# One kernel, five edits: the kv turn by transposes, the last attention step and the row of expert blocks laid anew

## The chip, the cores and the metric

The kernel runs on one core of a Trainium2 chip. The metric is device time: microseconds (us) from start to end of one execution, the median over several runs. The engines are named as in the profile: PE is TensorE's matmuls, PEld its loads of weights (the stationary operand), DVE is VectorE, ACT ScalarE, POOL GpSimd, SP SyncE, which here only issues DMAs. A q behind a name (SPq, POOLq) is that engine's queue of DMA issues and waits.

## The reference, cut to what matters

```python
# q, k, v: B=8, H=8, S=576, Dh=64; omega: M=128 random features
def phi(x):
    proj = einsum('bhsd,md->bhsm', x, omega)
    return concatenate([cos(proj), sin(proj)], -1) / sqrt(m)
kv  = einsum('bhsm,bhsd->bhmd', phi(k), v);  z = sum(phi(k), axis=s)
num = einsum('bhsm,bhmd->bhsd', phi(q), kv)
den = einsum('bhsm,bhm->bhs', phi(q), z)        # held away from zero
x = (num / den) as rows                          # N = B*S = 4608 tokens of 512
# experts: E=8, w1 (512 x 1024), w2 (1024 x 512)
logits = normalized(x) @ normalized(expert_emb).T / tau
expert = argmax(logits);  gate = softmax(logits)[expert]
out = gate * (relu(x @ w1[expert]) @ w2[expert])
```

## The kernel before, in words

**Attention: 32 steps.** A step n is one pair of heads of one batch (8 batches, NPAIR = 4 pairs). PE's order in a step n is written out by hand: the projection of q of step n, the output product `num` (line 373) of step n-1, the projection of k of step n+2, the turn of k of step n+3, `kv_products` of step n+1 and `kv_turn` of step n. The other engines follow in the order in which the calls stand: ScalarE moves projections out of PSUM and takes sines and cosines (`wave`, line 297), VectorE takes the fractional turns (line 278), folds them (`fold`, line 284) and copies PSUM, POOL adds up the sums over s (`zsum`, lines 309 to 314).

**kv_turn.** `kv_products` leaves kv with the 64 entries of a head's rows down the partitions, sine and cosine one above the other; VectorE copies it into `kvT`. `kv_turn` (lines 341 and 348) then turns it so that features lie on the partitions, and at the same time multiplies it by the normalized expert embeddings, to get logits along with the outputs. It does both by one product for each of two heads: the 128x128 `kvT` is the stationary operand, and `rmat`, 144 columns (2 x (64 + 8)), moves. `rmat` holds for each pair a unit block of 64 (which turns) and a block of 8 embedding columns. The unit blocks are written once at the start by POOL (`set_up_unit`, 8 copies, line 542), the embeddings by VectorE (`set_up_turn`). A second product of `zs` with the two columns of `zmask` turns the sums. All are fp32. `kv_out` copies the outcome from PSUM (`kvnew`) into SBUF as the weights of `num`.

**Rows.** `norm` divides and leaves rows in `xrow`; `store_rows` (line 425) writes them to DRAM as two DMAs of 288 KB for each two steps, and `store_logits` adds logits and token numbers, from which tokens are later fetched.

**Experts: blocks of 128 tokens of one expert.** `NBLK` is 43, of which NMAIN = 40 always run. Routing is done in two parts: blocks 0 to 10 hold tokens of the first batches, and blocks from K1 = 11 on those of the rest, whose places come out of `route_second` during blocks 1 to 6. For a block j, `gather` (POOL, line 910) fetches the rows by an indirect DMA into one of XBUF = 3 buffers; `ready` casts them to fp16 (`cast`, line 945 on ScalarE, 947 on POOL; a small copy of the logits on POOL comes with it) and turns them by a transposing DMA on SP's queue (line 1016); `square` (ScalarE, line 955) and `power` (POOL, line 964), `score`, `tanh` and `weigh` make the gate; `hidden_products` (line 1054, 32 matmuls, weights addressed by register) is the first layer, `clamp` its relu (the first half on ScalarE, line 1067, the second on VectorE, line 1069, or also on ScalarE in the first eight turns of the loop), `result_products` (line 1087, 8 matmuls) the second layer, `result_out` scales by the gate on ScalarE (line 1102) and scatters on POOL (line 1103). `square` frees the gather's buffer.

**The row of blocks** is one loop over j. Each turn issues, in this order: `hidden(j+1)` with its clamp, `score(j+1)` in odd j, `ready(j+4)` (cast on POOL for j+4 below 11, then on ScalarE), `result_products(j)`, `result_out(j)`, `square(j+4)`, `gather(j+6)`. In turn 1, the rows of the last pair of steps are stored on ScalarE's queue and its logits on SP's. An engine goes through its instructions in that order and waits in place.

**Change of stage.** The last step is written out ahead of the loop: `num(last - 1)`, sine of q, `hidden_products(0)` on PE, then `kv_turn(last)`, `fold` and cosine, `hot(0)` (a one-hot compare on VectorE, line 850, wanted by the routing of the second part), `kv_out(last)` on VectorE, and `num(last)`.

**PSUM** is one tile of eight banks of 512 words. The first layer of block 0 writes banks 0 and 1; `kvnew` lies at the end of bank 7, beside `num`'s bank.

## Time and profile before

| what | value |
|---|---|
| median of 3 runs | 453.14 us (452.38 to 454.96) |
| the profiled execution | 451.52 us, span 449.7 us |
| busy PE, PEld | 432.5 us (96%), 356.4 us (79%) |
| busy DVE, ACT, POOL | 327.5 us (73%), 344.0 us (76%), 370.0 us (82%) |
| moved by DMA | 80.32 MB, mean 179 GB/s |
| DMAs issued by POOL | 32 pieces of weights of 512 KB, 40 gathers, 40 scatters |

The span runs from the first instruction to the last; the execution's own time also has what lies around it, 1.8 us here. Busy times come from the instructions' own records; a matmul's end is modelled, so that a busy PE isn't PE at its peak. In rows of a timeline the first two numbers are start and length in us; a group of instructions one after the other is drawn into one row with its count (x2), and in brackets stands how long the engine stood idle before it and what it had waited for.

### The profile page before, as it was taken

What the parts mean: (1) busy time and instruction counts of PE and PEld (TensorE: products, weight loads), DVE (VectorE), ACT (ScalarE), POOL (GpSimd) and SP (SyncE); (2) the same over time, 40 slices, a digit from 0 to 9 for tenths busy, and PEclk for the clock granted to TensorE, in tenths of its full rate; (3) what the DMA queues carried; (4) which work ended last, traced back from release to release, by engine and by line L of the source; (5) the groups of instructions that cost most, each with busy time, mean ns of one, the idle gap of its engine ahead of it and who ended that gap; (6) DMA issues with size and microseconds to landing.
All of it is one profiled execution on the core that took longest, in us unless ns stands there. A gap on an engine that the chain in (4) does not pass through costs nothing. (4 is left out here: it accounts for less than half of the span.)

```text
span 449.7 us, 18881 instructions
## 1 busy us (share of the span) xinstructions
PE 432.5 (96%) x7799; PEld 356.4 (79%) x7799; DVE 327.5 (73%) x735; ACT 344.0 (76%) x478; POOL 370.0 (82%) x507
## 2 busy tenths in 40 slices
PE   8999999999999999999999999998999999999992
PEld 4788888989888888889888888876767777777770
DVE  5679977788777789898899989999753554554450
ACT  4878988888888889888888888875556777676741
POOL 8999998988889888889899898987877778777741
PEclk9999999999999999999999999999999999999997
DMA  7999998999999989999898896559577767777530
GB/s 193 200 203 206 205 202 195 194 182 212 200 195 209 197 191 202 188 212 192 176 229 190 177 203 111 102 123 204 149 161 200 183 147 202 164 202 168 151 91 30
DMA packets 80390, 80.32 MB, mean 179 GB/s; under 512 B 32678, under 2 KB 59302, under 8 KB 80304
## 3 DMA queue, kind: packets, MB, share of 16 engines
q1 hardware_dynamic: 59616, 42.59, 40.2%
q0 software_dynamic: 19200, 35.83, 39.3%
q8 instruction: 64, 1.05, 1.0%
q10 hardware_dynamic: 1488, 0.67, 0.7%
q14 instruction: 22, 0.18, 0.1%
HBM read 72.62 MB, written 20.09 MB: 206 GB/s over the span
## 5 line engine op out<-in xcount | busy, mean ns | idle before, releaser
L1054 PEld LDWEIGHTS <-w_sb 128*128 x1280 | 74.6, 98 | 12.5 <-issue 4.3
L373 PE MATMUL ps<-kv,siq 128*64 128x73 f32 x1152 | 76.6, 229 | 0.9 <-DVE gsc L973 0.9
L1087 PE MATMUL ps<-w_sb,coq 128*128 x320 | 75.6, 379 | 0.0
L373 PE MATMUL ps<-kv,coq 128*64 128x73 f32 x1152 | 75.0, 226 | 0.1
L373 PEld LDWEIGHTS ps<-kv,siq 128*64 128x64 f32 x1152 | 58.9, 135 | 12.9 <-issue 10.8
L373 PEld LDWEIGHTS ps<-kv,coq 128*64 128x64 f32 x1152 | 60.1, 137 | 0.2 <-issue 0.2
L278 DVE SCALAR_TENSOR_TENSOR cok<-cok,ps 128x128 f32<-128x128 f32 (+1 forms) x62 | 46.3, 748 | 13.0 <-ACT cok L272 13.0
L1087 PEld LDWEIGHTS <-coq 128*128 128x128 f16 x320 | 29.6, 98 | 28.8 <-DVE coq L1069 0.6
L910 POOL DMA_INDIRECT xin_all<-rf_x,prm x40 | 42.0, 1051 | 11.9 <-issue 8.1
L309 POOL TENSOR_TENSOR zt<-sik 128x384 f32<-128x384 f32 x31 | 39.6, 1277 | 12.8 <-ACT sik L297 12.1
L278 DVE SCALAR_TENSOR_TENSOR coq<-coq,ps 128x1152 f32<-128x1152 f32 x32 | 43.2, 1351 | 5.8 <-ACT coq L272 5.6
L297 ACT ACTIVATE siq<-coq 128x1152 f32<-128x1152 f32 x32 | 37.3, 1164 | 8.3 <-DVE coq L278 7.9
L297 ACT ACTIVATE cok<-cok,pio 128x1152 f32<-128x1152 f32 x31 | 38.9, 1255 | 5.1 <-DVE cok L284 5.0
L251 PE MATMUL ps<-qr,omT 32*128 32x288 f32 x512 | 41.5, 428 | 0.9 <-DVE kvT L334 0.5
L1054 PE MATMUL ps<-qr,w_sb 128*128 128x128 f16 x640 | 39.0, 219 | 3.1 <-DMA qr<-v 2.8
L945 ACT ACTIVATE v<-xin_all 128x512 f16<-128x512 f32 x32 | 20.1, 629 | 27.8 <-issue 15.2
L238 PE MATMUL ps<-omT,kT 64*128 64x128 f32 x522 | 40.7, 284 | 0.6 <-DVE coq L278 0.6
L297 ACT ACTIVATE coq<-coq,pio 128x1152 f32<-128x1152 f32 x32 | 40.2, 1256 | 1.3 <-DVE coq L284 1.2
L314 POOL TENSOR_TENSOR zs<-zs,zt 128x128 f32<-128x128 f32 x64 | 36.2, 566 | 5.0
L1054 PE MATMUL ps<-qx,w_sb 128*128 128x128 f16 x640 | 39.0, 219 | 0.1
L272 ACT ACTIVATE cok<-ps 128x1152 f32<-128x1152 f32 x31 | 35.0, 1129 | 4.6 <-POOL zt L312 1.0
L284 DVE TENSOR_SCALAR cok<-cok 128x1152 int32<-128x1152 int32 x31 | 27.7, 892 | 14.6 <-ACT sik L297 14.1
(214 smaller groups left out, 1171.0 us busy)
## 6 DMA issues: line engine op xcount, KB each, us to landing
w_sb<-in_moe_w_dram POOLq DMA_DIRECT2D x32, 512.0 KB, 8.0
qr<-in_q_dram SPq DMA_DIRECT2D x64, 144.0 KB, 4.9
rf_x<-xb SPq DMA_DIRECT2D x30, 288.0 KB, 4.6
kr<-in_k_dram SPq DMA_DIRECT2D x58, 144.0 KB, 4.7
v<-in_v_dram SPq DMA_DIRECT2D x32, 144.0 KB, 4.6
xin_all<-in_v_dram SPq DMA_DIRECT2D x30, 144.0 KB, 4.9
w_sb<-in_k_dram SPq DMA_DIRECT2D x6, 144.0 KB, 3.1
xin_all<-rf_x,prm POOLq DMA_INDIRECT x40, 3.7
```

What stands on the lines that cost most here:

```text
L238: nc.tensor.matmul(kreg[:, KS[c] * P : KS[c] * P + P], lhsT=t[r0 : r0 + 64, j * P : j * P + P], rhs=omT2[r0 : r0 + 64], start=True, stop=True,
L251: nc.tensor.matmul(qreg[:, g // 2, QW * (g % 2) : QW * (g % 2) + QW], lhsT=omT4[r0 : r0 + 32, b], rhs=t[r0 : r0 + 32].rearrange("p (c b j) ...
L272: nc.scalar.activation(dst, src, AF.Copy, bias=CMAGIC, scale=1.0)
L278: nc.vector.scalar_tensor_tensor(out=dst, in0=dst, scalar=CMAGIC, in1=src, op0=ALU.subtract, op1=ALU.subtract)
L284: nc.vector.tensor_scalar(t, t, 0x7FFFFFFF, None, ALU.bitwise_and)
L297: nc.scalar.activation(st[n][which + nm], t, AF.Sin, bias=pio2 if which == "co" else 0.0, scale=-TWO_PI * SINSC,)
L309: nc.gpsimd.tensor_tensor(zt, t[:, 0:3], t[:, 3:6], ALU.add)
L314: nc.gpsimd.tensor_tensor(z, z, zt[:, 2], ALU.add)
L373: nc.tensor.matmul(nm[r0 : r0 + 64, c], lhsT=ph[:, 2 * QW * hh + 64 * c : 2 * QW * hh + 64 * c + 64], rhs=d["kv"][:, hh, half], start=(hal ...
L910: ins = nc.gpsimd.indirect_dma_start(out=t, out_offset=None, in_=x_rows[:], in_offset=bass.IndirectOffsetOnAxis(ap=prm[:, j : j + 1], axis=0),
L1054: nc.tensor.matmul(h_ps[:, f * P : f * P + P], lhsT=weights(k), rhs=d["xT"][:, c * P : c * P + P], start=(c == 0), stop=(c == 3),)
L1087: nc.tensor.matmul(y_ps, lhsT=d["hT"][:, c * P : c * P + P], rhs=weights(NW1 + c), start=(c == 0), stop=(c == NW2 - 1),)
```

## The change

Five edits, in the order of the diff.

1. `rmat` keeps only the embedding columns, and `set_up_unit` is gone. `kv_turn` first transposes the two halves of `kvT` on PE against `ident` into the places of the head's rows in `kvnew`, then multiplies by 16 columns of embeddings.
2. The last step. `fold(last)` writes into another tile (apart) and stands right behind the sine, and the cosine behind it. `kv_turn(last)` lies in the middle of the first layer of block 0, after 12 of its 32 matmuls, into bank 2 (`kvlast`), and `kv_out(last)` stands ahead of `hot(0)`.
3. The store of the last rows is split: one half in turn 3, one in turn 5, both on ScalarE's queue behind that turn's clamp. The logits stay in turn 1.
4. The casts of blocks 8 and 10 run on ScalarE, behind `result_out` of their turn, with their transposing DMA there.
5. From turn 12 on a loop of its own. The whole clamp is on VectorE (but for the last block, where it is halved as before), `score(j+1)` stands ahead of `hidden(j+1)`, `square(j+4)` ahead of the cast, and the gather of block j+6 is issued ahead of the scatter of block j and waits for the last matmul of block j's second layer (`behind`). After the scatters of blocks 35, 36 and 37 stands a `drain` on POOL.

```diff
-    rmat = persist.tile([P, NPAIR, 2, 2, 64 + E], FP32)
+    rmat = persist.tile([P, NPAIR, 2, 2, E], FP32)
...
+        kvlast = ps[:, 2 * 512 : 2 * 512 + 4 * W].rearrange("p (h a w) -> p h a w", h=2, a=2)
...
-        def fold(n, nm):
+        def fold(n, nm, apart=False):
             t = st[n]["co" + nm].bitcast(I32)
-            nc.vector.tensor_scalar(t, t, 0x7FFFFFFF, None, ALU.bitwise_and)
+            if apart:
+                st[n]["co" + nm] = pa.tile(
+                    [P, NCH * P], FP32, tag="co" + nm, name="co" + nm, bufs=2
+                )
+            nc.vector.tensor_scalar(
+                st[n]["co" + nm].bitcast(I32), t, 0x7FFFFFFF, None, ALU.bitwise_and
+            )
...
-        def kv_turn(n):
+        def kv_turn(n, kvnew=kvnew):
             b, i = steps[n]
             d = st[n]
+            d0, e0 = (E, 0) if i % 2 == 0 else (0, 64)
+            for a in range(2):
+                nc.tensor.transpose(kvnew[:, a, :, d0 : d0 + 64], d["kvT"][:, a], ident)
             for a in range(2):
                 nc.tensor.matmul(
-                    kvnew[:, a, :, 0 : W - 1],
+                    kvnew[:, a, :, e0 : e0 + E],
                     lhsT=d["kvT"][:, a],
                     rhs=rmat[:, i, a],
...
-        def store_rows(b, a, eng=nc.sync):
-            t = xrow.pop((b, a))
-            for hh in range(2):
+        def store_rows(b, a, eng=nc.sync, halves=(0, 1)):
+            t = xrow.pop((b, a)) if 1 in halves else xrow[b, a]
+            for hh in halves:
...
-        def set_up_unit():
-            for half in range(2):
-                r0 = 64 * half
-                for a in range(2):
-                    d0 = E if a == 0 else 0
-                    for h2 in range(2):
-                        nc.gpsimd.tensor_copy(
-                            rmat[r0 : r0 + 64, a::2, h2, half, d0 : d0 + 64],
-                            ident[r0 : r0 + 64, r0 : r0 + 64]
-                            .unsqueeze(1).to_broadcast([64, NPAIR // 2, 64]),
-                        )
...
-        set_up_unit()
...
+        STEADY = 12
+        LATE = (8, 10)
...
-            nc.scalar.activation(hT[:, 0:512], h_ps[:, 0:512], AF.Relu)
+            if eng != "all":
+                nc.scalar.activation(hT[:, 0:512], h_ps[:, 0:512], AF.Relu)
             if eng == "act":
                 nc.scalar.activation(hT[:, 512:], h_ps[:, 512:], AF.Relu)
+            elif eng == "all":
+                nc.vector.tensor_scalar(hT, h_ps, 0.0, None, ALU.max)
             else:
...
         wave(last, "si", "q")
+        fold(last, "q", apart=True)
+        wave(last, "co", "q")
         square(1)
         power(0, 2)
         norm(last - 1)
-        hidden_products(0)
+        hidden_products(0, range(12))
+        kv_turn(last, kvlast)
+        hidden_products(0, range(12, NW1))
         expert_of(1)
-        kv_turn(last)
-        fold(last, "q")
-        wave(last, "co", "q")
         gather(3)
         sums_even(*end)
         gather(4)
         ready(2, "act")
+        kv_out(last, "dve", kvlast)
         hot(0)
-        kv_out(last, "dve")
...
-        for j in range(NMAIN):
+        for j in range(STEADY):
...
-            if m < NMAIN:
+            if m < NMAIN and m not in LATE:
                 ready(m, "act" if m >= K1 else "pool")
...
             elif j == 1:
-                store_rows(*end, eng=nc.scalar)
                 store_logits(NGRP - 1)
+            elif j in (3, 5):
+                store_rows(*end, eng=nc.scalar, halves=(j // 4,))
             result_products(j)
...
+            if m in LATE:
+                ready(m, "act")
             if m < NMAIN:
                 square(m)
             if g < NMAIN and g != K1:
                 gather(g)
...
+        for j in range(STEADY, NMAIN):
+            m, g = j + 4, j + 6
+            if j % 2 == 0:
+                tanh(j, 2)
+                weigh(j, 2)
+            elif j + 1 < NMAIN:
+                score(j + 1, 2)
+            if j + 1 < NMAIN:
+                hidden(j + 1, "all" if j + 2 < NMAIN else "dve")
+            if m < NMAIN:
+                square(m)
+                ready(m, "act")
+            if j % 2 == 0 and j + 2 < NMAIN:
+                power(j + 2, 2)
+            done = result_products(j)
+            if g < NMAIN:
+                behind(gather(g), done)
+            result_out(j)
+            if NMAIN - 6 < j < NMAIN - 2:
+                nc.gpsimd.drain()
```

## Rows read from the trace of the kernel before

**Rows 1.** The page's busy time of each engine, share of the span, instructions.

```profile
PE 432.5 (96%) x7799; PEld 356.4 (79%) x7799; DVE 327.5 (73%) x735; ACT 344.0 (76%) x478; POOL 370.0 (82%) x507
```

**Rows 2.** Busy time by windows: stretch, length, engines (instructions), PE clock, DMA share, GB/s.

```profile
150.00:160.00 10.00, 10.00 (x232) 8.90 (x227) 7.74 (x11) 8.90 (x10) 9.33 (x12) 1.00 0.93 190
...
400.00:410.00 10.00, 10.00 (x119) 7.47 (x118) 4.37 (x20) 7.17 (x17) 8.17 (x11) 1.00 0.74 173
```

**Rows 3.** PE's weight loads in time: start, us, line, tiles; two steps' kv_turn.

```profile
58.75 0.30 PEld L341 LDWEIGHTS ps<-rmat,kvT 128*128 128x128 f32 x2 [0.17 <-DVE cok L278]
...
67.51 0.30 PEld L341 LDWEIGHTS ps<-rmat,kvT 128*128 128x128 f32 x2 [0.17 <-DVE cok L278]
```

**Rows 4.** The same view, one whole kv_turn and the load after it.

```profile
270.68 0.30 PEld L341 LDWEIGHTS ps<-rmat,kvT 128*128 128x128 f32 x2 [0.17 <-DVE cok L278]
270.91 0.31 PEld L348 LDWEIGHTS ps<-zmask,zs 128*128 128x128 f32 x2
271.14 0.30 PEld L341 LDWEIGHTS ps<-rmat,kvT 128*128 128x128 f32 x2
...
271.71 0.31 PEld L251 LDWEIGHTS ps<-qr,omT 32*128 32x128 f32 x8
```

**Rows 5.** The same view, set-up: two loads of 128x128, then the next line's.

```profile
5.18 0.20 PEld L591 LDWEIGHTS ps<-ident,w_sb 128*128 128x128 f32 x2
5.35 0.21 PEld L531 LDWEIGHTS <-ident 128*128 128x128 bf16 x2
```

**Rows 6.** POOL's instructions in time, set-up.

```profile
3.18 2.10 POOL L542 COPY rmat<-ident 64x128 f32<-64x128 f32 x8
...
8.47 2.03 POOL L514 TENSOR_TENSOR w_sb<-w_sb,emb_n 8x512 f32<-8x512 f32 x2 [0.44 <-DVE emb_n L512]
```

**Rows 7.** PE's matmuls in time: first layers of blocks 0, 5, 9; `num(last)`.

```profile
291.01 1.95 PE L1054 MATMUL ps<-qr,w_sb 128*128 128x128 f16 x32 [0.24 <-DVE coq L278]
...
294.79 0.35 PE L373 MATMUL ps<-kv,siq 128*64 128x73 f32 x4 [0.95 <-DVE gsc L973]
...
313.54 1.95 PE L1054 MATMUL ps<-qr,w_sb 128*128 128x128 f16 x32 [1.73 <-DMA qr<-v]
...
329.75 1.95 PE L1054 MATMUL ps<-qr,w_sb 128*128 128x128 f16 x32 [1.10 <-DMA qr<-v]
```

**Rows 8.** VectorE and ScalarE in time, the last step.

```profile
292.92 1.35 DVE L850 TENSOR_TENSOR oh<-io_p,ar 128x1152 f16<-128x1152 f16 x1
...
294.19 0.45 DVE L203 COPY kv<-ps 128x292 f32<-128x292 f32 x1
...
293.04 1.25 ACT L297 ACTIVATE coq<-coq,pio 128x1152 f32<-128x1152 f32 x1 [0.21 <-DVE coq L284]
```

**Rows 9.** Stores, a transposing DMA and POOL's cast in time, blocks 2 to 6.

```profile
303.01 1.34 ACTq L425 DMA_DIRECT2D rf_x<-xb  x2
...
306.30 3.06 SPq L1016 DMA_TRANSPOSE qr<-v  x1
...
310.96 0.61 POOL L947 CAST v<-xin_all 128x512 f16<-128x512 f32 x1 [1.99 <-DMA xin_all<-rf_x,prm]
```

**Rows 10.** The end's line 1420: duration min/median/max in ns, first and last start.

```profile
L1420 POOLq DRAIN  x3: 46/103/5215, 443.7 to 449.5; - x3
...
L1420 SPq DRAIN  x3: 7/7/13, 445.1 to 449.2; - x3
```

**Rows 11.** Line 1406, the program's start, the same columns.

```profile
L1406 POOLq DRAIN  x1: 168/168/168, 0.3 to 0.3; - x1
```

**Rows 12.** POOL and PE in time, blocks 35 to 39.

```profile
429.68 1.06 POOL L1103 DMA_INDIRECT out_dram<-siq,ptk  x1 [1.57 <-ACT siq L1102]
...
434.17 0.73 POOL L964 TENSOR_TENSOR gsc<-gsc,half 128x2 f32<-128x2 f32 x1
...
437.32 3.62 PE L1087 MATMUL ps<-w_sb,coq 128*128 x16
```

**Rows 13.** Groups by line and shape: busy us, mean ns, idle before, its releaser.

```profile
L1069 DVE TENSOR_SCALAR coq<-ps 128x512 f16<-128x512 f32 x31 | 20.7, 679 | 11.3 <-PE ps L1054 11.3
```

More of the change, by code (lines that the diff above doesn't have):

```diff
@@ L354, in kv_turn, with kv_out @@
                 )
-        def kv_out(n, eng="act"):
+        def kv_out(n, eng="act", kvnew=kvnew):
             kv = pa.tile([P, 2, 2, W], FP32, tag="kv", name="kv", bufs=2)
@@ L552, in set_up_turn @@
                 for a in range(2):
-                    e0 = 0 if a == 0 else 64
-                    nc.vector.tensor_copy(
-                        rmat[r0 : r0 + 64, a::2, :, half, e0 : e0 + E], emb_t[r0 : r0 + 64, a::2]
+                        nc.vector.tensor_copy(
+                        rmat[r0 : r0 + 64, a::2, :, half], emb_t[r0 : r0 + 64, a::2]
                     )
@@ L921, in gather @@
             xin[j] = t
+            return ins
         def bank(k, cols=512):
@@ L1047, in weights, with hidden_products @@
             return w2b[:, ds(at - W2BASE, 1024)].bitcast(FP16)
-        def hidden_products(j):
+        def hidden_products(j, ks=range(NW1)):
             d = mo[j]
             h_ps = bank(4 * (j % 2), 1024)
-            for k in range(NW1):
+            for k in ks:
                 f, c = k // 4, k % 4
@@ L1086, in result_products @@
             for c in range(NW2):
-                nc.tensor.matmul(
+                d["done"] = nc.tensor.matmul(
                     y_ps,
@@ L1097, in result_products @@
                     place(j + 1, range(NW1 + 6 * (c - 6), min(NW1 + 6 * (c - 5), NW1 + NW2)))
+            return d["done"]
         def result_out(j):
@@ L1368, with behind @@
                 block_experts(K1, NBLK - K1, True, r2["a"])
+        def behind(ins, first):
+            tc.add_manual_dep(
+                ins.ins,
+                first.ins.name,
+                mybir.DependencyInfo(mybir.DependencyClass.Sync, mybir.DependencyReason.DATA),
+                reason="rows are called for as a second layer ends",
+            )
+        for j in range(STEADY, NMAIN):
[18 more added lines that the diff above has]
+                nc.gpsimd.drain()
             if j == 20:
```

## The prediction, made before the changed kernel was run

> **What bounds the kernel now.** I read four views, in this order. First the page's busy shares: TensorE (PE) is busy 96% of the span, no other engine above 82% [rows 1]. Second, busy time by stretches of 10 us: in the attention steps PE shows 10.00 of 10, and in the late blocks again [rows 2], so in both stages only work taken from PE, or put on it, moves the end. Third, PE's own timeline. The weight loads of one line start at 58.75 and again at 67.51 [rows 3]: a step lasts 8.76 us, and nearly all 31 steps have that length, which is how an engine looks that waits for nobody. PE stands still for others only around the change of stage: 0.95 us before num of the last step, 1.73 and 1.10 us before two first layers (blocks 5 and 9), both for a turned block, "DMA qr<-v" [rows 7]; 3.78 us in all. Fourth, the end: the other queues are through at 445.1 us, POOL's last DRAIN begins at 443.7 and takes 5.2 [rows 10], so it alone holds the end until 448.9. So there are three places where time can go or come from: the PE work of the 31 steps, the waits around the change of stage, the last drain.
>
> **kv_turn by transposes (adds).** Now a step's kv_turn holds four fp32 products of two passes each, eight weight loads, and lasts 270.68 to 271.71 = 1.03 us [rows 4]. The pair of loads for the 144-column product takes 0.23 (270.68 to 270.91); the pair for the two-column product takes 0.23 as well (to 271.14) [rows 4]. The loads set the pace, not the columns, so cutting 144 columns to 16 saves next to nothing: at most the 0.01 or so by which a 144-column pass outlasts a load, four times, 0.04. What is added is two transposes of 128x128. Their nearest row is the set-up pair of the same shape: its first load starts at 5.18, the next line's load at 5.35, 0.17 [rows 5]. So a step grows by 0.17 - 0.04 = 0.13, at most by 0.17, at least by 0.115. A gain is excluded by the two-column pair: with almost no columns it is no cheaper. Thirty steps of 0.126: **+3.8 us** (3.5 to 5.1). Nothing covers it, since PE is what the step waits for. The price of the turn is also on the Trainium skill's page "TensorE: Matmul & The Clock Gate", section "LDWEIGHTS (loading the stationary operand)": load time is columns over 1.2, some 107 ns for 128. By it the two turns would not start 0.06 apart but 0.107, the step would grow by 0.175 and the time would be about 452.3 (an estimate from that page). The pair in the rows has both its loads, 0.14 each, done within 0.20 [rows 5], which speaks against it, and the row decides.
>
> **No unit blocks in rmat (removes).** Eight POOL copies, 2.10 us, at 3.18, and most of two memsets [rows 6]. They are not on the path as a whole: POOL then waits 0.44 for VectorE before the expert scaling at 8.47 [rows 6], and that input does not come more than that earlier. Yet POOL is the busiest of the other engines [rows 1], and the sums of the first steps stand in its queue behind this, so some of its lead can reach PE. I take **-0.4** (0 to -0.4).
>
> **Last step (moves).** kv_out of the last step stands on VectorE behind hot(0): that runs 292.92 to 294.28, kv_out 294.19 to 294.65, and num starts at 294.79 [rows 7, 8]. Moved ahead of hot(0) and with its product inside the first layer of block 0, kv_out can end near 293.3; the fold into another tile lets the cosine follow the sine at about 292.2 instead of 293.04 [rows 8], so it ends by 293.5. PE itself gets there last: the first layer starts at 291.01 and lasts 1.95 [rows 7], with about 1.0 of kv_turn inside it now: 293.9, against 294.79. Gain 0.9, rounded down for the change of tile shape: **-0.85**. What is pushed back: the square of block 1 and with it POOL's power and gather of block 3 by about a microsecond; blocks 3 to 5 then have about 1 us to spare rather than 2.5.
>
> **Stores in blocks 3 and 5, casts 8 and 10 (moves).** The two stores of 288 KB are issued by ScalarE at 303.01; behind them block 5's transpose sits 3.06 us in SP's queue instead of 1.2, and POOL's cast of block 6 waits 1.99 us for its gather [rows 9]. That is the 1.73 us of block 5. The stores now follow in halves, each on ScalarE's queue behind the casts and clamps of its block and ahead of that block's result; each shares the DMA engines with a transpose and a gather of a later block, for half as long. The casts taken from POOL (0.6 each) shorten the queue that feeds block 9, but ScalarE, in order, then waits for gathers 8 and 10 with the next clamp behind it, and PE behind that. I count block 5 at -1.4, block 9 at -0.65 and 0.3 for a new wait at block 6 or 7: **-1.75**. Bounds for all waits around the change of stage: -3.8 (all gone) and -0.9 (the last step alone). Taken: **-2.6**.
>
> **Blocks from 12 on.** Whole clamp on VectorE (two times 0.68 [rows 13]), gather before scatter, gather behind the last second-layer product. PE is full there, and 119 matmuls in 10 us at 40 a block make 3.4 to 3.5 us for a block [rows 2]. The new wait is for PE itself; behind it on POOL stand that block's scatter and the next block's copy and power, needed a block and more later. **0**, at a cost of its own only if a gather then lands more than a block late.
>
> **Drains.** POOL's first drain of the program, with no DMA behind it, took 0.168 us, and the second and third of the end 0.103 and 0.046 [rows 10, 11]; the 5.2 us one has all of POOL's 112 DMAs behind it (32 pieces of weights, 40 gathers, 40 scatters). So I take it that a drain pays for what was issued since the one before. Three early ones then leave the last one almost nothing: the end moves to the other queues' 445.1, 3.8 us less. The first, after the scatter of block 35 (429.68 to 430.74), may still take 5.0: then power runs from 435.7 to 436.5 instead of 434.17 [rows 12], and since score(38) now stands ahead of clamp(38) on VectorE, that clamp (1.35) ends at 438.4, where PE wants it at 437.32 [rows 12]: 1.1 us, with a little more for block 39. Between -2.5 and -3.8 I take the middle, **-3.1**.
>
> **Sum.** 3.8 - 0.4 - 2.6 - 3.1 = -2.3 us. The profiled execution took 451.52 us (span 449.7 and 1.8 around it), 1.6 below the median of the runs shown, 453.14; the difference is carried onto the median: **450.8**.
>
> **Rivals.** (A) The last drain stays as long, because it pays for something that is there at every end. For it: the row shows one length only. Then the end gives 0: 453.14 + 3.4 - 2.6 = 453.9. (B) Slower: every drain costs what the last one does. POOL is free from 430.74, drains to 435.9, power and scatter 36 to 437.7, drain to 442.9, scatter 37, drain to 449.1, two more scatters to 451.1, against 442.9 now: +8.2, so 462.1. It decides from about 2.4 us a drain, what a block of 3.5 leaves beside a scatter. Against it: 0.1 us for a second drain [rows 10]. (C) The waits of blocks 5 and 9 only move: half a store beside block 7's or 9's transpose, and ScalarE, with two casts more, late with the clamps. Then the change of stage gives 0.9: 452.5. In its favour speaks the Trainium skill's page "DMA: Bandwidth & Descriptors", section "Issuing engines are not separate DMA queues": transfers of all issuers share the same 16 engines; by that the stores cost the same wherever they go, and the trace so far shows only that they collide. (D) The transposes are free, because their loads slip under the products before: 447.0. Against it: eight loads now show no gap to slip into [rows 4].
>
> **How the numbers follow.** Forecast 0.52 (its own range 448.2 to 453.2), A 0.18, B 0.10, C 0.10, D 0.10. About 0.5%, 2.3 us, is what a measurement of this kernel can tell from no change: faster means below 450.9, slower above 455.4. The forecast lies on that edge: 0.33 of its 0.52 faster, 0.19 within. A gives 0.10 within and 0.08 slower, B 0.10 slower, C 0.09 within and 0.01 faster, D 0.10 faster. Sums: 0.44, 0.38, 0.18. The range reaches from D to A with the dearest turn and the least gain at the change of stage (5.1 - 0.9 would be 457, taken in to 456): 447.6 to 456.0; it leaves out B and the tails.
>
> **What the new profile would show.** Right: steps of 8.88 to 8.90 us; two single-pass loads ahead of the fp32 pairs; num of the last step without a wait; no long transpose in SP's queue near block 5; a last drain under 1 us and one long one near block 35. Wrong: steps still of 8.76 (D); a last drain of 5 us (A), or three of them (B); waits for "DMA qr<-v" or "qx<-v" at blocks 6 to 10 as long as those that went (C).

## The result: slower by 1.1 to 1.4%, and the profile after

The changed kernel takes 461.17 us in the median beside 454.96 for the kernel before in the same session, a ratio of 1.0137 with an interval of 1.0097 to 1.0178: 6.2 us slower. Measured once more in another session it was 1.0107 (1.0054 to 1.016), 4.9 us. The forecast was 450.8 with a range to 456.0. The profiled execution of the first session took 466.95 us, with TensorE's clock at 0.70 of full from 280 to 290 us, so the rows of after are those of the second session's profile, an execution of 458.58 us (span 456.8).

The page's busy time of the changed kernel, to be read against [rows 1]:

```profile
PE 437.3 (96%) x7863; PEld 360.5 (79%) x7863; DVE 342.6 (75%) x735; ACT 331.6 (73%) x454; POOL 366.6 (80%) x497
```

PE has 64 instructions and 4.8 us more work; it still bounds the kernel. Its weight loads in one kv_turn, and the start of the next step's, answer to [rows 3, 4]:

```profile
59.74 0.20 PEld L349 LDWEIGHTS ps<-ident,kvT 128*128 128x128 f32 x2 [0.17 <-DVE cok L279]
59.91 0.30 PEld L351 LDWEIGHTS ps<-rmat,kvT 128*128 128x128 f32 x2
60.13 0.30 PEld L358 LDWEIGHTS ps<-zmask,zs 128*128 128x128 f32 x2
60.35 0.30 PEld L351 LDWEIGHTS ps<-rmat,kvT 128*128 128x128 f32 x2
60.58 0.30 PEld L358 LDWEIGHTS ps<-zmask,zs 128*128 128x128 f32 x2
60.90 0.31 PEld L252 LDWEIGHTS ps<-qr,omT 32*128 32x128 f32 x8
...
68.63 0.20 PEld L349 LDWEIGHTS ps<-ident,kvT 128*128 128x128 f32 x2 [0.17 <-DVE cok L279]
```

kv_turn lasts 60.90 - 59.74 = 1.16 us, and was 1.03; a step lasts 68.63 - 59.74 = 8.89, and was 8.76. The pair of transposes takes 0.17, and the 16-column pair 0.22 where the 144-column pair took 0.23. That is the whole account of a step: 0.17 more, 0.04 less over the four products that are left.

POOL's set-up, in time (start, length, in brackets the idle time before and what ended it), answers to [rows 6]:

```profile
6.87 0.58 POOL L516 TENSOR_TENSOR emb_n<-emb_n,half 8x1 f32<-8x1 f32 x1 [2.85 <-DVE w_sb L511]
8.11 1.03 POOL L524 TENSOR_TENSOR w_sb<-w_sb,emb_n 8x512 f32<-8x512 f32 x1 [0.65 <-DVE emb_n L522]
```

The 2.10 us of copies are gone, and POOL stands idle for 2.85 us in their place: it waits for VectorE. Its expert scaling starts at 8.11 in place of 8.47, 0.36 us earlier; VectorE's first operation of the attention steps, on line 279, does not come forward by it (11.71, and 11.59 before).

PE's matmuls answer to [rows 7]: `num(last)`, the first product of the second part's routing (line 728), and the first layer of block 6 and the second layer of block 13, with PE's longest waits there. The transposing DMA of block 6 in SP's queue and half a store in ScalarE's answer to [rows 9]:

```profile
300.58 0.35 PE L383 MATMUL ps<-kv,siq 128*64 128x73 f32 x4
...
311.07 0.20 PE L728 MATMUL ps<-cumx,onesb 128*128 128x80 bf16 x1 [0.67 <-DVE cumx L723]
323.25 1.95 PE L1053 MATMUL ps<-qx,w_sb 128*128 128x128 f16 x32 [1.36 <-DMA qx<-v]
356.55 1.89 PE L1089 MATMUL ps<-w_sb,coq 128*128 x8 [1.91 <-DVE gsc L973]
```

```profile
316.61 1.19 SPq L1015 DMA_TRANSPOSE qx<-v  x1
...
316.76 0.59 ACTq L435 DMA_DIRECT2D rf_x<-xb  x1
```

`num(last)` no longer waits, and its 0.95 us is gone. But the routing product now waits 0.67 us for `cumx`, a running sum that VectorE makes. The wait for a turned block has moved from block 5 (1.73) to block 6 (1.36): block 6's transposing DMA lies only 1.19 us in SP's queue, but the first half of the split store is issued 0.15 us behind it, and the block is there only when PE starts at 323.25. At block 13 there is a wait that the kernel before didn't have, 1.91 us for VectorE. The rows of the whole clamp, of what stands ahead of it, and of PE's first weight load of that second layer:

```profile
351.34 0.17 DVE L974 TENSOR_SCALAR gsc<-gsc 128x2 f32<-128x2 f32 x1 [2.64 <-POOL gsc L963]
...
353.54 0.18 DVE L986 TENSOR_SCALAR gsc<-gsc 128x16 f32<-128x16 f32 x1 [1.62 <-ACT gsc L980]
...
354.77 1.20 DVE L1069 TENSOR_SCALAR coq<-ps 128x1024 f16<-128x1024 f32 x1
```

```profile
356.03 0.10 PEld L1089 LDWEIGHTS <-coq 128*128 128x128 f16 x1 [1.56 <-DVE coq L1069]
```

VectorE waits for `power` (POOL, 2.64), then for `tanh` (ScalarE, 1.62), does `weigh`, and only then the clamp of 1.20 us, in which ScalarE now has no half. The clamp ends at 355.97, the weight load starts at 356.03, and the first product 0.52 us after it, at 356.55; so PE's own row names an instruction of VectorE that came later (line 973), and not the clamp.

The drains in the kernel (line 1404) and at the end (line 1456), with duration min/median/max in ns and first and last start, answer to [rows 10]; below them POOL's last rows in time:

```profile
L1404 POOLq DRAIN  x3: 3263/4071/6115, 436.5 to 447.1; - x3
L1456 POOLq DRAIN  x3: 46/109/2316, 453.1 to 456.5; - x3
```

```profile
436.73 0.98 POOL L1106 DMA_INDIRECT out_dram<-siq,ptk  x1 [2.22 <-ACT gsc L980]
442.71 0.72 POOL L963 TENSOR_TENSOR gsc<-gsc,half 128x2 f32<-128x2 f32 x1 [5.00 <-issue]
443.63 1.04 POOL L1106 DMA_INDIRECT out_dram<-sik,ptk  x1 [0.20 <-ACT siq L1105]
447.34 0.98 POOL L1106 DMA_INDIRECT out_dram<-siq,ptk  x1 [2.67 <-issue]
451.97 0.97 POOL L1106 DMA_INDIRECT out_dram<-sik,ptk  x1 [3.66 <-issue]
453.25 0.97 POOL L1106 DMA_INDIRECT out_dram<-siq,ptk  x1 [0.30 <-DMA out_dram<-siq,ptk]
```

A drain's record begins before the scatter ahead of it has been issued, so its price is read from the idle time of the instruction behind it: 5.00, 2.67 and 3.66 us. (A drain's end less the end of the scatter's issue ahead of it, which is used below, is 4.9, 1.8 and 2.9.) The last drain did fall, from 5.2 to 2.3 us. But the last scatter is issued at 453.25, after PE's last matmul had ended at 448.86; in the kernel before the two stood at 441.93 and 440.93. From PE's last matmul to the end of the span it is 7.92 us, in place of 8.80: the end gained 0.9 us, and PE lost as much to a clamp that waits for `power(38)`.

### The profile page after: what moved, and what is told of

The parts are those of the page before. It is cut to its first block, busy times and chain, and to the rows that moved or that the text cites. A ratio compares the mean times of both kernels' runs of the same rounds, so it can differ in the third digit from the quotient of the medians.

```text
span 465.2 us, 18984 instructions
## 1 busy us (share of the span) xinstructions
PE 443.2 (95%) x7863; PEld 364.9 (78%) x7863; DVE 341.3 (73%) x735; ACT 331.8 (71%) x454; POOL 366.7 (79%) x497
## 5 line engine op out<-in xcount | busy, mean ns | idle before, releaser
L1053 PEld LDWEIGHTS <-w_sb 128*128 x1280 | 75.6, 99 | 12.6 <-issue 4.6
L383 PE MATMUL ps<-kv,siq 128*64 128x73 f32 x1152 | 78.0, 231 | 0.0
L383 PE MATMUL ps<-kv,coq 128*64 128x73 f32 x1152 | 76.2, 228 | 0.0
L383 PEld LDWEIGHTS ps<-kv,siq 128*64 128x64 f32 x1152 | 59.9, 137 | 12.4 <-issue 11.2
L908 POOL DMA_INDIRECT xin_all<-rf_x,prm x40 | 43.1, 1077 | 19.6 <-PE ps L1089 7.7
L316 POOL TENSOR_TENSOR zt<-sik 128x384 f32<-128x384 f32 x31 | 41.1, 1327 | 20.6 <-ACT sik L304 20.2
L289 DVE TENSOR_SCALAR cok<-cok 128x1152 int32<-128x1152 int32 x31 | 30.1, 971 | 18.3 <-ACT sik L304 17.7
L316 POOL TENSOR_TENSOR zt<-cok 128x384 f32<-128x384 f32 x32 | 36.5, 1142 | 2.9 <-ACT cok L304 0.6
L1069 DVE TENSOR_SCALAR coq<-ps 128x1024 f16<-128x1024 f32 x26 | 31.6, 1214 | 9.0 <-PE ps L1053 9.0
```

What stands on the lines that cost most here:

```text
L289: nc.vector.tensor_scalar(st[n]["co" + nm].bitcast(I32), t, 0x7FFFFFFF, None, ALU.bitwise_and)
L316: nc.gpsimd.tensor_tensor(zt, t[:, 0:3], t[:, 3:6], ALU.add)
L383: nc.tensor.matmul(nm[r0 : r0 + 64, c], lhsT=ph[:, 2 * QW * hh + 64 * c : 2 * QW * hh + 64 * c + 64], rhs=d["kv"][:, hh, half], start=(hal ...
L908: ins = nc.gpsimd.indirect_dma_start(out=t, out_offset=None, in_=x_rows[:], in_offset=bass.IndirectOffsetOnAxis(ap=prm[:, j : j + 1], axis=0),
L1053: nc.tensor.matmul(h_ps[:, f * P : f * P + P], lhsT=weights(k), rhs=d["xT"][:, c * P : c * P + P], start=(c == 0), stop=(c == 3),)
L1069: nc.vector.tensor_scalar(hT, h_ps, 0.0, None, ALU.max)
```

## The experiments

Ratios are against the kernel before in the same session, whose median was 455.0 to 458.5 us in the six sessions; us are what the ratio makes of that median (1.0107 of 455.55 is +4.9). "Lag" is the start of an instruction less its start in the trace ahead of the prediction.

**again.** The changed kernel, nothing edited.

> The changed kernel once more, to see which of its differences come back. Theory 1 (the loss is the sum of PE work and waits that the order sets): about 7 us over the kernel before; steps of 8.89 us against 8.76; 2.8 us of waiting of the second layer of block 13 for a clamp on VectorE, as in the first profile, and no lower clock where PE has worked without a gap. Theory 2 (the wait at block 13 and the late steps 27 to 29 are chance, from one execution): steps of 8.89 again, but no wait over 1 us after block 12, and 4 us over the kernel before.

Measured: 1.0107 (1.0054 to 1.016), +4.9 us. The wait at block 13 is there again, 1.91 us, in an execution without a lower clock; so theory 2 falls by its wait; the time alone (+2.5 to +7.3) couldn't tell the two apart. The lag grows by 0.13 in most steps of the attention (0.58 at step 3, 3.99 at step 25), by 2.7 in the last six, where PE waits 1.10 us for VectorE at step 26 and 0.95 at step 28, falls by 1.3 from block 0 to block 11 (6.66 to 5.38), grows by 1.9 at block 13 and is the same at block 37 and at the end of the span (7.06 and 7.05).

**turn_only.** Edit 1 on the kernel before.

```diff
-    rmat = persist.tile([P, NPAIR, 2, 2, 64 + E], FP32)
+    rmat = persist.tile([P, NPAIR, 2, 2, E], FP32)
+            for a in range(2):
+                nc.tensor.transpose(kvnew[:, a, :, d0 : d0 + 64], d["kvT"][:, a], ident)
-        set_up_unit()
```

> The kernel before with the kv turn by transposes alone (and without the unit blocks). Theory 1: 0.13 us more for each of 31 steps, 4.0 us; nothing back at the start, since POOL waited 3.6 us for VectorE in the changed kernel where its copies were: +4.0 us. The first estimate had 3.4 (3.8 less 0.4 at the start). Rival: the step only grows where other edits take the slack away: within 1 us of the kernel before.

Measured: 1.0103 (1.0063 to 1.0143), +4.7 us. Its weight loads show the step of the changed kernel:

```profile
68.95 0.20 PEld L342 LDWEIGHTS ps<-ident,kvT 128*128 128x128 f32 x2 [0.17 <-DVE cok L278]
...
77.84 0.20 PEld L342 LDWEIGHTS ps<-ident,kvT 128*128 128x128 f32 x2 [0.17 <-DVE cok L278]
```

8.89 us, so 31 times 0.13, 4.0, with no other edit beside it. The rest of the 4.7 is inside the interval (2.9 to 6.5), but the traces show a place for some of it: in the last steps PE waits longer with the new turn. From step 25 to block 0, where five dearer turns are worth 0.65 us, the lag grows by 1.8 here, 2.6 in `again` and 1.9 in row_undone (by 7.1 and 9.3 in the two other profiles with the new turn, with a lower clock there); in 12 of the 14 with the old turn it grows by 1.0 at most, in two by 2.2 and 2.5. Why the new turn brings these waits stays open. The turn alone costs about as much as the whole change.

**drains_only.** The three drains on the kernel before.

```diff
+            if NMAIN - 6 < j < NMAIN - 2:
+                nc.gpsimd.drain()
```

> The kernel before with the three drains after the scatters of blocks 35, 36 and 37 alone. In the changed kernel they took 4.9, 1.8 and 2.3 us from the end of the scatter before, the last one 1.2, and the last scatter left 2.8 us late. Theory 1 (a drain waits for the scatter in flight, about 2 us each time, and the first one also for what has piled up, 3 to 4 us): the end moves by -0.5 us (-1.5 to +0.7). The estimate on record, that drains two and three are nearly free: -3.1. Rival, each costs as much as the last one did, 5.2: +8.

Measured: 1.0005 (0.9974 to 1.0035), +0.2 us. POOL and PE, in time:

```profile
439.97 1.89 PE L1087 MATMUL ps<-w_sb,coq 128*128 x8
...
442.35 0.72 POOL L964 TENSOR_TENSOR gsc<-gsc,half 128x2 f32<-128x2 f32 x1 [1.93 <-issue]
443.26 1.03 POOL L1103 DMA_INDIRECT out_dram<-siq,ptk  x1 [0.19 <-issue]
...
444.61 3.31 PE L1087 MATMUL ps<-w_sb,coq 128*128 x8 [2.75 <-ACT coq L1065]
...
448.92 0.98 POOL L1103 DMA_INDIRECT out_dram<-siq,ptk  x1 [0.99 <-POOLq L1377]
```

`power(38)`, which stands behind two drains in the old row, comes at 442.35, against 434.17 [rows 12]. `score`, `tanh` and, behind `tanh` on ScalarE, the clamp of block 39 follow it, and PE waits 2.75 us for that. Its eight products then take 3.31 us in place of 1.89, for the granted clock falls from full (2.4 GHz) to half (1.2 GHz); the columns are stretch, length, PE (instructions), PE clock, DMA share and GB/s:

```profile
442.00:445.00 3.00, 0.39 (x2) 1.00 0.05 20
445.00:448.00 3.00, 2.92 (x7) 0.50 0.20 75
```

From block 37 to PE's last matmul the lag grows by 4.3 us, 2.75 of waiting and 1.6 of the lower clock; behind that matmul the end takes 5.9 us in place of 8.8. In the median nothing of that is left as a gain.

**row_undone.** The changed kernel with the old row from turn 12 on, the three drains kept.

```diff
-        for j in range(STEADY):
+        for j in range(NMAIN):
...
-        for j in range(STEADY, NMAIN):
```

> The changed kernel with the row from turn 12 in the old loop: clamp halved, score behind hidden, scatter ahead of gather, no wait of a gather for PE; all else as changed, the three drains too. Theory 1: the second layer of block 13 no longer waits for a whole clamp that stands behind a score and a weigh on VectorE: 2.5 to 4 us less than the changed kernel. Rival (the wait is only the lateness of the stage change that ends there, whatever the order): the same wait shows at a block between 11 and 15, and the time is within 1 us of the changed kernel.

Measured: 1.0049 (1.0018 to 1.008), +2.2 us, 2.6 less than the changed kernel beside it. The waits at blocks 14 and 13 don't go, but are 0.57, 0.50 and 0.23 us in place of 1.91. So a part of the lateness is there with the old row too, and the new row makes more of it; where it comes from isn't shown. With the old row PE also waits 2.77 us at block 39, as in drains_only, where the changed kernel waits 0.69 at block 38.

**one_drain.** One drain on the kernel before.

```diff
+            if j == NMAIN - 5:
+                nc.gpsimd.drain()
```

> The kernel before with one drain, behind the scatter of block 35. Theory (a drain takes the time until the scatter ahead of it has landed, 1.8 us behind its issue, and once some 3 us more for what POOL had issued since the last drain): the drain takes 4.9 us behind its scatter, delays block 36's scatter by 3 us and nothing that PE waits for by more than 0.5 us, and the drain at the end falls from 6.0 us behind the last scatter to about 2: -3.5 us. Rival (the 3 us are owed again at the end, or a drain makes what follows late, as with three): 0, with a last drain of 5 us, or with a wait of the second layer of block 38 or 39.

Measured: 0.9941 (0.9912 to 0.997), -2.7 us. The drain (line 1370) and the end's (line 1422):

```profile
L1370 POOLq DRAIN  x1: 6212/6212/6212, 438.1 to 438.1; - x1
L1422 POOLq DRAIN  x3: 46/109/1694, 452.5 to 455.2; - x3
```

From the end of its scatter's issue, 439.40, to 444.30 the drain takes 4.9 us, as with three; the last one falls to 1.7. One drain is worth what three are not.

**stage_only.** Edits 2, 3 and 4 on the kernel before, as the diff ahead of the prediction has them.

> The kernel before with edits 2, 3 and 4 alone: the last step laid anew, the stores in turns 3 and 5, the casts of blocks 8 and 10 on ScalarE. On record: -2.6. Theory after the two first runs: the last step's 0.9 is real, but the waits for turned blocks only move, to block 6 in place of block 5, about 1.4 us: -1.3 us against the kernel before, whose own waits for turned blocks differ by up to 2 us between executions. Rival: nothing moves but the place, within 0.5 us.

Measured: 0.9956 (0.9927 to 0.9984), -2.0 us. PE ahead of block 6:

```profile
318.12 1.95 PE L1064 MATMUL ps<-qx,w_sb 128*128 128x128 f16 x32 [0.94 <-DMA qx<-v]
```

The lag falls by 1.0 from block 0 to block 1, and by 0.9 to 1.0 in each of the eleven profiled executions with edit 2, while without it it falls in none of the eight. But it comes back ahead of block 3, where the second part's routing waits for `cumx` of VectorE. PE and VectorE here, then in the kernel before:

```profile
306.02 0.20 PE L739 MATMUL ps<-cumx,onesb 128*128 128x80 bf16 x1 [0.73 <-DVE cumx L734]
305.19 0.78 DVE L734 TENSOR_TENSOR_SCAN cumx<-keep,eq 128x296 bf16<-128x296 bf16 x1
...
304.54 0.20 PE L732 MATMUL ps<-cumx,onesb 128*128 128x80 bf16 x1
303.31 0.77 DVE L727 TENSOR_TENSOR_SCAN cumx<-keep,eq 128x296 bf16<-128x296 bf16 x1
```

`cumx` ends 13.1 us behind the start of block 0 in both; PE, which came 0.45 us behind it before, now comes first and waits. It does so by 0.6 to 1.0 us in ten of the eleven, and from block 0 to block 3 their lag changes by -0.05 in the mean (-0.4 to 0.75). From block 3 to block 11 it then changes by -0.2 in the mean of the eleven (-1.2 to 1.8) and by +0.8 in that of the seven others and the trace ahead of the prediction (0 to 2.1; drain_early left out). The waits for turned blocks add up to 1.9 us there in the mean of the eleven (0.9 to 2.7) and to 2.4 in that of the others (1.4 to 3.8). So the traces give some 1 us in all, and none of it that stays to the last step; the time (-3.3 to -0.7) has room for that and for the -2.6 on record.

**turn_undone.** The changed kernel with the old kv turn.

```diff
-    rmat = persist.tile([P, NPAIR, 2, 2, E], FP32)
+    rmat = persist.tile([P, NPAIR, 2, 2, 64 + E], FP32)
-            for a in range(2):
-                nc.tensor.transpose(kvnew[:, a, :, d0 : d0 + 64], d["kvT"][:, a], ident)
+        set_up_unit()
```

> The changed kernel with the old kv turn, 144 columns and unit blocks; all else as changed. Theory: steps of 8.76 again, 4.0 to 4.7 us less than the changed kernel, that is about the time of the kernel before (-1 to +1). Rival (the changed kernel loses by its waits, and the steps would only wait elsewhere): less than 2 us of it come back.

Measured: 0.9975 (0.9951 to 0.9999), -1.1 us; against +4.9 with the turn, 6.0 came back, more than the theory had; the waits in the last steps (turn_only) are one place for it. The two were measured in different sessions, and their intervals together allow 3 to 9.

**turn_undone_drain34.** As before, with one drain.

```diff
-            if NMAIN - 6 < j < NMAIN - 2:
+            if j == NMAIN - 6:
                 nc.gpsimd.drain()
```

> The changed kernel with the old kv turn and one drain behind the scatter of block 34 in place of the three. Theory: the drain ends before power(38), so that no clamp waits for it; the last drain is 2 us: 3.5 to 4 us less than with the old turn and three drains, and 3.5 to 5 us less than the kernel before. Rival (the drain is owed again at the end): the same as with three, within 0.7 us.

Measured: 0.9919 (0.9891 to 0.9947), -3.7 us: 2.6 better than with three drains beside it. PE doesn't wait at blocks 36 to 39 (the lag is 5.42 us from block 37 to PE's last matmul).

**stage_old_row_drain35** and **stage_old_row_drain34.** stage_only with one drain, behind block 35 or block 34.

```diff
+            if j == NMAIN - 5:
+                nc.gpsimd.drain()
```

> The kernel before with edits 2, 3 and 4 and one drain behind the scatter of block 35; neither the turn by transposes nor the new row. Theory (the gains add: -2.0 for the change of stage, -2.7 for the drain): -4.7 us against the kernel before. Rival (the two meet, because what comes earlier out of the change of stage is lost to a wait in the blocks): no better than one drain alone, -2.7.

> As the one before, with the drain behind the scatter of block 34. Theory: in the old row power(36) and with it score(36) and tanh(36) stand behind this drain, so that the clamp of block 37 comes 1 us late, but the drain begins 3.5 us earlier and the last scatter is on time: within 1 us of the drain behind block 35. Rival (whatever is late at a drain, PE waits for it in full): 2 to 3 us more than behind block 35.

Measured: 0.99 (0.9859 to 0.9941), -4.6 us, and 0.9919 (0.9879 to 0.9959), -3.7. The gains of the change of stage and of the drain add. Behind block 34 PE waited 2.28 us for a clamp on ScalarE at block 37 in the profiled execution, as the rival had it, but the two times can't be told apart.

**row_only.** Edit 5 on the kernel before, without drains.

> The kernel before with the new row from turn 12 alone, without a drain: whole clamps on VectorE, score ahead of hidden, gather ahead of scatter and waiting for PE. On record: 0. Theory (the whole clamp stands behind score and weigh, which wait for power and tanh; a wait of 0.3 to 2 us of a second layer at block 13 or 15): +0.9 us, between 0 and +2.6. Rival (the old row loses as much there, at other blocks): within 0.5 us.

Measured: 1.0043 (1.0008 to 1.0078), +2.0 us. PE at block 13, and the two clamps on VectorE:

```profile
353.00 1.89 PE L1100 MATMUL ps<-w_sb,coq 128*128 x8 [1.54 <-DVE gsc L984]
```

```profile
351.43 1.20 DVE L1080 TENSOR_SCALAR coq<-ps 128x1024 f16<-128x1024 f32 x1
...
353.55 1.22 DVE L1080 TENSOR_SCALAR coq<-ps 128x1024 f16<-128x1024 f32 x1
```

The wait of the changed kernel is there with the new row alone.

**row_half.** The same with halved clamps.

```diff
-                hidden(j + 1, "all" if j + 2 < NMAIN else "dve")
+                hidden(j + 1, "dve")
```

> The kernel before with the new row from turn 12, without drains, but with halved clamps as in the old row. Theory 1 (the new row costs by whole clamps on VectorE, 1.2 us that stand behind weigh and score when POOL is late): 1.0 to 1.9 us less than with whole clamps, that is within 1 us of the kernel before. Theory 2 (it costs by the order, score ahead of the clamp and gathers that wait for PE, so that each block's gather lands later): as with whole clamps, +1.9.

Measured: 0.9983 (0.9961 to 1.0005), -0.8 us (-1.8 to +0.2), 2.7 less than with whole clamps (+0.4 to +3.6), in another session. That is theory 1's side, and more than it had: the cost of the new row is the whole clamp, and the order without it costs nothing that can be measured. No second layer from block 12 on waits over 0.3 us here.

**stage_drain_power38** and **drain_power38.** One drain behind `power(38)`, with edits 2 to 4 and alone.

```diff
                 if j >= K1:
                     power(j + 1, 2)
+                if j == NMAIN - 3:
+                    nc.gpsimd.drain()
```

> The kernel before with edits 2, 3 and 4 and one drain, set behind power(38) and ahead of the scatter of block 37, where nothing that PE waits for stands behind it on POOL. Theory (the time that drains cost PE comes from power(38) alone, for which score, tanh, weigh and the clamps wait): no wait of a second layer at blocks 37 to 39, the scatters catch up by block 39, and the last drain takes 2 to 3 us: -2.0 for the change of stage and -3.3 for the drain, -5.3 us against the kernel before. Rival (the wait at block 39 with the drain behind block 35 has another cause, or the drain is owed again at the end): no better than behind block 35, -4.2.

> The kernel before with that one drain behind power(38) alone. Theory: -3.3 us, against -2.7 behind block 35 and 0 with three. Rival: a drain this late leaves three scatters queued behind it, the last one is issued 2 us late or more, and nothing is won: 0.

Measured: 0.9926 (0.9899 to 0.9954), -3.4 us, and 0.9941 (0.9917 to 0.9965), -2.7. PE's wait at block 39 is gone in both (the lag is the same from block 37 to PE's last matmul), so it was `power(38)` that carried it. But the time is no better than behind block 35. POOL in drain_power38:

```profile
447.34 1.03 POOL L1103 DMA_INDIRECT out_dram<-siq,ptk  x1 [5.81 <-ACT sik L1102]
448.67 0.97 POOL L1103 DMA_INDIRECT out_dram<-sik,ptk  x1 [0.30 <-POOLq L1377]
449.95 0.97 POOL L1103 DMA_INDIRECT out_dram<-siq,ptk  x1 [0.30 <-issue]
```

The drain stands in the 5.81 us of idle time ahead of the first row, and the last scatter comes at 449.95, where PE's last matmul had ended at 447.55: what PE no longer waits, the scatters wait. With edits 2 to 4 the -5.3 of the theory lies outside the interval (-4.6 to -2.1); alone, -3.3 lies inside (-3.8 to -1.6). So a larger gain isn't shown, and the places of one drain that were tried can't be told apart.

**drain_early** and **drain_ladder.** The kernel before with drains behind more or fewer transfers.

```diff
+        nc.gpsimd.drain()
         last = NS - 1
...
+            if j in (12, 20, 24, 26, 27, 28):
+                nc.gpsimd.drain()
```

> The kernel before with a drain at the end of the attention steps (behind it 32 pieces of weights and 4 gathers) and one behind the scatter of block 35 (behind it 36 gathers and 36 scatters). Only the lengths of the drains are asked for; the time grows since gathers wait. With one drain behind block 35 and 108 transfers issued before, it took 4.9 us behind the end of its scatter's issue. Theory P (a drain pays 0.03 us for each transfer issued since the last one, and 1.8 for the one in flight): the early one 1.0 us beyond its flight, the second 1.8 + 2.2 = 4.0. Theory Q (the first drain after transfers pays some 3 us, whatever their number, those after it nothing): the early one 3 us beyond its flight, the second 1.8. Theory R (it is the gathers and scatters that a drain pays for, not the pieces): the early one its flight alone, the second 4.9.

> The kernel before with six drains, each right behind a gather, after blocks 12, 20, 24, 26, 27 and 28: behind the first are 32 pieces, 19 gathers and 13 scatters, behind the others 16, 8, 4, 2 and 2 transfers. Only the lengths of the drains are asked for; the time grows. So far, behind the issue of the transfer ahead of it: 1.8 us with one transfer since the last drain, 4.0 with 36, 4.9 to 6.0 with 72 to 112. Theory P (so much for each transfer since the last drain, 0.03 to 0.06, up to a limit): lengths fall along the ladder, from 5 to 6 at the first to 2.5 to 3 (the flight of a gather) at the last two. Theory S (the length depends on what is in flight at that moment, not on how many came before): all six alike within 0.7 us.

Measured: in drain_early 4.0 us behind the end of the gather's issue with 35 transfers (three gathers had gone out by then, not four), then 6.0 behind a scatter's with 73; none of P, Q and R has both. On the ladder POOL's idle time behind the drains after blocks 12 and 27, with 64 and 2 transfers since the last drain:

```profile
356.39 0.72 POOL L964 TENSOR_TENSOR gsc<-gsc,half 128x2 f32<-128x2 f32 x1 [3.15 <-issue]
...
420.22 0.19 POOL L948 COPY gsc<-xin_all 128x9 int32<-128x9 int32 x1 [2.77 <-issue]
```

3.15 us with 64 transfers and 2.77 with 2: the number hardly matters here, and theory P falls. From the end of the gather's issue the six take 3.0, 3.3, 2.9, 2.8, 2.6 and 2.5, which is 0.8 apart where S allowed 0.7; S is the nearer one. But S doesn't tell why the drain at the end, behind a scatter, takes 6.0 with 112 transfers before it, 3.6 on the ladder with 16, and 1.2 to 2.6 with 2 to 5. What a drain's length goes by stays open.

**half_drain34** and **turn_half_drain34.** The changed kernel with halved clamps and one drain behind block 34, with the old and with the new kv turn.

> The changed kernel with the old kv turn, halved clamps in the new row, and one drain behind the scatter of block 34. Theory (the parts add: the change of stage -2.0, the new row with halved clamps -0.8, one drain -2.7): -5.5 us against the kernel before, 1.8 less than with whole clamps (-3.7). Rival (whole clamps cost only in the row without a drain): -3.7 again.

> The same with the kv turn by transposes, so the changed kernel but for the clamps and the number of drains. Theory (the turn is its own price, 4.0 to 4.7 us, whatever stands beside it): -0.8 us against the kernel before, between -1.5 and 0. Rival (the turn's price was partly the waits of the blocks, which halved clamps take away): 3 us or less over the kernel with the old turn beside it.

Measured: 0.9884 (0.9834 to 0.9934), -5.3 us, and 0.9968 (0.9933 to 1.0003), -1.5. The parts add up: -5.5 and -0.8 were expected. With all else equal and in one session the turn thus costs 3.8 us (some 1 to 6.6, by the two intervals). half_drain34 is faster than both kernels; it has the change of stage and the new row, with the old turn, halved clamps and one drain for three.

## Why the prediction was wrong, step by step

**Where the bound is** was right: PE, and three places. **kv turn:** the mechanism and the size of the step held. +3.8 was forecast, 30 times 0.126; the step grew by 0.13, and the runs give 3.8 and 4.7, each in one session, and 6.0 across two. The row of the set-up's pair, 0.17, gave the price to 0.01 us. The waits of the last steps, which the new turn lengthens, had no term. The Trainium skill's page "TensorE: Matmul & The Clock Gate", section "LDWEIGHTS (loading the stationary operand)", would have made the step 0.175 longer by an estimate from its columns over 1.2; this case's steps are 0.13 longer, so here the measurement decides against it. Rival D falls.

**No unit blocks:** -0.4 was forecast. The step took POOL's queue for the path; POOL waited for VectorE right behind, as [rows 6] already showed with a wait of 0.44, and the traces show nothing of a gain on PE. No run has this edit by itself, so that 0 is read from traces and not from a time.

**Last step:** -0.85 was forecast. The wait of `num(last)` went by the mechanism named and block 1 came 0.9 to 1.0 us earlier, but this step of the prediction ended its reckoning at `num(last)`: two blocks on, PE waits for `cumx`, which VectorE has no earlier than before, and by block 3 the gain is gone (-0.05 in the mean of eleven). **Stores and casts:** -1.75 was forecast; the traces show some 1 us between block 3 and block 11 (-0.2 against +0.8), and the time of both edits together is -2.0 (-3.3 to -0.7), in which the -2.6 on record still lies. What failed is the count of block 5 and block 9 as gains. The longest wait for a turned block was 0.9 to 2.6 us in executions of the old order, at block 4, 5, 8 or 9, and 0.8 to 2.7 in those of the new, at block 6 in ten of eleven. The wait moved for the most part, as rival C had it, though to another block: in all eleven the half store of turn 3 is issued within 0.7 us of block 6's transposing DMA. By the Trainium skill's page "DMA: Bandwidth & Descriptors", section "Issuing engines are not separate DMA queues", transfers of all issuers run on the same 16 DMA engines. The trace agrees, with the store on ScalarE's queue at 316.76 and the late block of SP's queue at 316.61; no run moved the store by itself.

**Blocks from 12 on:** 0 was forecast, +2.0 came. The step looked at the gathers, and in `again` no first layer after block 6 waits for a turned block. But it gave two clamps of 0.68 as equal to one whole clamp, and overlooked that ScalarE's half can start while VectorE is still held by `weigh` and `score`. The whole clamp is 1.20 us behind them, and where the blocks before come late, PE waits for it: at block 13, 0.3 to 2.8 us in all five profiles with whole clamps, where the others have 0.6 at most. From block 11 to block 37 the lag grows by 3.3 us in the mean of those five (1.3 to 4.8), by 1.0 in the three with the new row and halved clamps (-0.4 to 2.9) and by 1.6 in the eleven with the old row, the trace ahead of the prediction among them (-0.4 to 4.7; drain_ladder left out). Much of that spread is PE standing still inside first layers, up to 0.5 us at a time, for which the profile names no cause.

**Drains:** -3.1 was forecast, +0.2 came with three. This is the step that failed most. The 0.103 and 0.046 us of [rows 10] were drains with no transfer between them; a drain behind one scatter takes 1.8 to 2.9 us from the end of its issue, not 0.1. Rival B was right in kind: the three took 9.6 us of POOL (4.9, 1.8 and 2.9), and the last scatter came 4.4 us behind PE's last matmul in place of 1.0. What lies behind PE's last matmul fell from 8.8 to 7.9 us, where the forecast let it fall by 3.8. The forecast's long drain at block 35 was right (4.9 against 5.0), and so was the clamp that waits for `power(38)` (0.9 us of PE in `again`, 1.1 forecast). Rival A falls: the last drain became shorter in each run with one ahead of it, and one drain alone wins 2.7. With the old turn, one drain behind block 34 is 2.6 us better than the three (turn_undone_drain34 against turn_undone).

**Sum.** In place of 3.8 - 0.4 - 2.6 + 0 - 3.1 = -2.3 the parts by themselves measure 4.7 (the turn without unit blocks) - 2.0 + 2.0 + 0.2 = +4.9, and the whole 4.9 and 6.2. Of the 7.2 us between -2.3 and +4.9, 3.3 are the drains, 2.0 the row from block 12 on, 0.6 the change of stage and 1.3 the turn with its set-up. The range failed since its upper end held each term's bound but took the row as free and gave three dear drains (B) a tenth. The trace ahead of the prediction was also a short execution: in 17 of the 19 others profiled, step 0 began 0.7 to 2.6 us later, of which 0.2 to 1.7 were left by step 5 in 12 of the 14 with the old turn, and the medians of the kernel before were 455.0 to 458.5, not 453.14. The ratios carry none of this.

## What to carry to other kernels

Take a duration from a row only with what stood ahead of it: a drain with nothing in flight says nothing about one behind a transfer. An instruction that moves whole from two engines to one has the later of the two queues ahead of it, so look at what holds that queue when the stage before is late, not at the sum of durations. A gain counts only as far as the engine's next wait: follow it past the place where it arises, here to the routing two blocks on. And where one profiled execution shows a wait for a DMA, its size is one draw; count on the place, and give the size the spread of several executions.

## What was not expected of the hardware

Drains took 2.5 to 4.0 us behind a gather and 1.2 to 6.0 behind a scatter; why the two differ stays open. And in the first profile of the changed kernel the granted clock fell after PE had stood still for 2.3 us, to a mean of 0.70 over 10 us, between its levels of 2.4 and 1.2 GHz:

```profile
270.00:280.00 10.00, 7.68 (x165) 0.96 0.82 159
280.00:290.00 10.00, 10.00 (x181) 0.70 0.19 54
```

The columns are those of drains_only above. In the second execution PE had 9.05 us of work in the first of these windows, and the clock stayed at 1.00. This is no single case: behind the set-up the clock fell to 0.5 while PE still had work in 11 of the 20 profiles, each time in or behind a wait of PE of 1.75 to 4.25 us, in drains_only and row_undone at block 39, in half_drain34 at block 6. The wait of 2.75 us in drains_only cost 4.3. So a wait there can cost more than its own length.
